# A fused attention and GeGLU kernel: from 512-token chunks with hand-placed pieces to 128-token tiles ordered by a list scheduler

## Chip, cores, metric

One core of one Trainium2 chip. The metric is the device time of one execution in microseconds (us). Each kernel was executed several times; "median" is over those executions. An execution counts as slow when it is more than 1.5% above the fastest of the same kernel; only fast ones are compared.

## The reference

A pre-LayerNorm block: multi-query attention (2048 tokens, width 640, 32 heads of 20, one K and V head shared by all), then a gated feed-forward part of width 1536. All in bf16.

```python
def _A_ref(x, wq, wk, wv, wo):            # attention; H = 32, Dh = 20
    q = (x @ wq).reshape(B, S, H, Dh).transpose(0, 2, 1, 3)
    k = x @ wk
    v = x @ wv
    scores = jnp.einsum("bhqd,bkd->bhqk", q, k) * (Dh ** -0.5)
    p = _softmax(scores, axis=-1)
    o = jnp.einsum("bhqk,bkd->bhqd", p, v)
    return o.transpose(0, 2, 1, 3).reshape(B, S, H * Dh) @ wo
def _B_ref(x, w_gate, w_up, w_down):
    return (_gelu(x @ w_gate) * (x @ w_up)) @ w_down
h  = x + _A_ref(_layernorm(x), ...)       # no affine in the LayerNorm
h2 = h + _B_ref(_layernorm(h), ...)       # (cut: rounding, shapes)
```

The exponentials set the scale: 32 x 2048 x 2048 values are 1024 instructions of 128x1024 on ScalarE.

## The kernel before

Attention runs in 512 steps. A step is one chunk of 512 queries, one group of four heads and one tile of 128 keys. A head has only 20 channels, so four heads share the matmul array in two ways. For QK each head takes 32 of the 128 rows: four matmuls with `tile_position=(32*r, 0)` run side by side (in the trace the four start within about 10 ns and are over after 0.39 us at full clock, 0.61 at half). For PV each head takes 32 of the 128 columns (0.40 and 0.62 us for the four). The kernel uses eight banks of PSUM: three pairs for scores, one for PV, and bank 7 for everything else.

```python
PAIRS = [(0, 1), (2, 3), (4, 5)]            # score banks: three slots of two
def qk_fn(e, s):                            # all four heads of a step together
    qc, g, kt = steps[s]
    pa, pb = pair_of_step[s]
    for half, pr in ((0, pa), (1, pb)):
        for rr in range(2):
            r = 2 * half + rr
            ins = e.matmul(bank(PAIRS[pr][rr]),
                kT4[32*r:32*r+32, kt*P:(kt+1)*P], qT[32*r:32*r+32, qc % 2, g, :],
                start=True, stop=True, tile_position=(32*r, 0))
    return ins
# per step: exp of pair a, exp of pair b (ScalarE, 128x1024 each),
#           qk_fn of the next step, pv_fn (four matmuls into bank 6),
#           then at most one "piece" (2 or 3 matmuls of a projection or of the FFN)
# ... (cut: pieces of one unit follow each other step by step; the FFN of the last
#      chunk runs after the attention; softmax sums by a matmul and 512-wide reciprocals)
```

The softmax here doesn't subtract the row's maximum and nothing guards it: scores larger than these inputs give would overflow.

## Time and profile before

| | before |
|---|---|
| median of 2 executions | 1118.51 us (1117.74 to 1119.27) |
| ScalarE busy | 978.6 us, 88% of the span |
| TensorE busy | 760.8 us, 68% |
| first exponential starts, last one starts | 29.6 us, 1013.5 us |
| after the last exponential | about 103 us |
| half-rate TensorE clock during the exponentials | 368 of 984 us |

The page of the profile gives each engine's busy time; then 40 equal slices of the span with the busy share of each in tenths (9 is 90% or more); PEclk is the clock granted to TensorE, in tenths of full speed. Then comes the chain of waits that ended last, by engine and line, and groups of instructions: count, then busy us and mean ns, then how long the engine stood idle before them and what released it.

```profile
PE 760.8 (68%) x5424; PEld 204.0 (18%) x5508; DVE 457.8 (41%) x693; ACT 978.6 (88%) x1088; POOL 80.4 (7%) x104
...
PE   1677666666667776666777777767766766766866
...
ACT  0799999999899999999999999999999999993030
...
PEclk9799655555899999755999999985997699966998
...
ACT 74%; DVE 16%; PE 9%; issue 1%; DMA 1%; POOL 0%; another core or an unknown queue 0%
...
L475 ACT ACTIVATE scratch_a<-ps 128x1024 bf16<-128x1024 f32 x1024 | 950.5, 1132 | 24.2 <-PE ps L462 23.3
...
L462 PE MATMUL ps<-qT,kT 32*128 32x512 bf16 x2048 | 243.0, 464 | 83.6 <-ACT scratch_a L475 77.5
```

ScalarE is the limit: it carries 74% of the chain and stands only 24.2 us before its 1024 exponentials. One lasts 1132 ns on average, but they overlap and start about every 917 ns. TensorE's clock is only half in parts of the attention, as the timeline of TensorE in such a stretch shows (columns: start, duration, engine, line, what, and how long it stood before):

```profile
200.06 0.61 PE L462 MATMUL ps<-qT,kT 32*128 32x512 bf16 x4 [0.30 <-ACT scratch_a L475]
200.98 0.62 PE L481 MATMUL ps<-scratch_a,v_ext 128*32 128x512 bf16 x4 [0.30 <-ACT scratch_a L475]
201.90 0.61 PE L462 MATMUL ps<-qT,kT 32*128 32x512 bf16 x4 [0.30 <-ACT scratch_a L475]
```

TensorE waits for ScalarE ahead of every group, even at half clock. The view of stretches of time confirms it (us busy of each engine in the stretch, then the granted clock): ScalarE is busy 10.00 of 10 us.

```profile
core 0: us, PE busy (x) PEld busy (x) DVE busy (x) ACT busy (x) POOL busy (x), PEclk, DMA share, GB/s
200.00:210.00 10.00, 6.78 (x44) 1.22 (x44) 0.00 (x0) 10.00 (x13) 0.00 (x0) 0.50 0.00 0
```

### The profile page before, as it was taken

To read this page: it belongs to the slowest core of one execution; us is meant where nothing else is said; L and a number is where in the kernel's file an instruction comes from. 1 tells how busy PE (TensorE), PEld (TensorE's weight loads), DVE (VectorE), ACT (ScalarE), POOL (GpSimd) and SP (SyncE) were. 2 spreads that over 40 slices of the span, in tenths; PEclk is the share of its full clock that TensorE was granted. 3 is DMA by queue.
4 is the path that set the end of the run, shared out by engine and by line. 5 is a ranking of instruction groups with operands and counts; after the bars stand their busy time and mean duration, and the time that the engine had idled before them with its cause. 6 is when DMAs were issued, how large, how long until landed. Compare 5 with 4: busy or idle time off the path is not lost.

```text
span 1117.3 us, 13050 instructions
## 1 busy us (share of the span) xinstructions
PE 760.8 (68%) x5424; PEld 204.0 (18%) x5508; DVE 457.8 (41%) x693; ACT 978.6 (88%) x1088; POOL 80.4 (7%) x104
## 2 busy tenths in 40 slices
PE   1677666666667776666777777767766766766866
PEld 0121111111121111111221111111221111112322
DVE  7433222211164656421224455642333356533573
ACT  0799999999899999999999999999999999993030
POOL 5200000000000111000000011100000011100130
PEclk9799655555899999755999999985997699966998
DMA  5460000000000000000000100000000000000100
GB/s 155 91 216 1 1 1 1 1 1 1 1 16 9 1 1 1 1 1 0 19 6 1 24 1 1 1 1 1 19 6 18 6 2 1 1 1 1 48 0 24
DMA packets 31772, 18.92 MB, mean 17 GB/s; under 512 B 23520, under 2 KB 30432, under 8 KB 31712
## 3 DMA queue, kind: packets, MB, share of 16 engines
q1 hardware_dynamic: 31712, 18.08, 5.9%
q8 instruction: 43, 0.70, 0.3%
q14 instruction: 17, 0.14, 0.0%
HBM read 10.21 MB, written 2.62 MB: 11 GB/s over the span
## 4 chain that ended last, share of the span: by engine, by line
ACT 74%; DVE 16%; PE 9%; issue 1%; DMA 1%; POOL 0%; another core or an unknown queue 0%
ACT scratch_a L475 72%; DVE rL_sb L527 4%; PE ps L778 2%; ACT g_th L719 2%; PE ps L672 2%; DVE g_z L713 2%; DVE hhT L733 1%; DVE g_hg L725 1%; PE ps L481 1%; PE ps L462 1%; DVE stats L277 1%; DVE stats L272 1%; PE ps L970 1%; DVE onT L531 1%; DVE xn_tmp L323 1%
## 5 line engine op out<-in xcount | busy, mean ns | idle before, releaser
L475 ACT ACTIVATE scratch_a<-ps 128x1024 bf16<-128x1024 f32 x1024 | 950.5, 1132 | 24.2 <-PE ps L462 23.3
L481 PE MATMUL ps<-scratch_a,v_ext 128*32 128x512 bf16 x2048 | 245.9, 470 | 192.9 <-ACT scratch_a L475 186.4
L462 PE MATMUL ps<-qT,kT 32*128 32x512 bf16 x2048 | 243.0, 464 | 83.6 <-ACT scratch_a L475 77.5
L481 PEld LDWEIGHTS ps<-scratch_a,v_ext 128*32 128x32 bf16 x2048 | 54.2, 95 | 382.4 <-ACT scratch_a L475 375.9
L509 DVE COPY opvT<-ps 128x512 f32<-128x512 f32 x32 | 22.1, 692 | 247.5 <-PE ps L481 247.5
L462 PEld LDWEIGHTS ps<-qT,kT 32*128 32x128 bf16 x2048 | 53.2, 94 | 313.6 <-ACT scratch_a L475 299.3
L527 DVE RECIPROCAL rL_sb<-rL_sb 128x512 f32<-128x512 f32 x32 | 107.3, 3353 | 1.1
L707 POOL TENSOR_TENSOR g_sq<-g_gs 128x512 bf16<-128x512 bf16 x48 | 53.3, 1111 | 372.1 <-DVE g_gs L700 332.5
L672 PE MATMUL ps<-xnT,wg_sb 128*128 128x512 bf16 x220 | 65.5, 401 | 15.3 <-DVE hhT L733 9.9
L672 PE MATMUL ps<-xnT,wu_sb 128*128 128x512 bf16 x228 | 66.2, 395 | 6.9 <-DVE g_gs L700 5.0
L778 PE MATMUL ps<-wd_sb,hhT 128*128 128x512 bf16 x185 | 53.6, 422 | 11.2 <-DVE hhT L733 7.2
L767 DVE CAST g_us<-ps 128x512 bf16<-128x512 f32 x36 | 24.9, 691 | 80.1 <-PE ps L672 79.7
L297 POOL TENSOR_TENSOR ln_den<-ln_ve,halfc 128x4 f32<-128x4 f32 x8 | 8.1, 1010 | 637.9 <-DVE ln_ve L295 622.6
L719 ACT ACTIVATE g_th<-g_z 128x512 bf16<-128x512 bf16 x48 | 34.6, 721 | 19.1 <-DVE g_z L713 19.1
L702 ACT ACTIVATE g_gs<-ps 128x512 bf16<-128x512 f32 x12 | 7.2, 597 | 48.5 <-PE ps L672 48.5
L525 DVE COPY rL_sb<-ps 128x512 f32<-128x512 f32 x32 | 22.0, 689 | 60.2 <-PE ps L481 53.3
L413 DVE CAST qT<-ps 128x512 bf16<-128x512 f32 x31 | 21.4, 689 | 56.6 <-PE ps L591 56.6
L700 DVE CAST g_gs<-ps 128x512 bf16<-128x512 f32 x36 | 24.8, 689 | 41.6 <-PE ps L672 41.6
L713 DVE SCALAR_TENSOR_TENSOR g_z<-g_sq,g_gs 128x512 bf16<-128x512 bf16 x48 | 39.6, 825 | 4.2 <-POOL g_sq L707 4.2
L725 DVE SCALAR_TENSOR_TENSOR g_hg<-g_th,g_gs 128x512 bf16<-128x512 bf16 x48 | 33.3, 695 | 10.9 <-ACT g_th L719 10.9
L733 DVE SCALAR_TENSOR_TENSOR hhT<-g_hg,g_us 128x512 bf16<-128x512 bf16 x36 | 31.4, 871 | 1.2
L616 PE MATMUL ps<-wo_pad,onT 128*128 128x512 bf16 x88 | 28.3, 397 | 4.9 <-DVE onT L531 3.6
(69 smaller groups left out, 362.4 us busy)
## 6 DMA issues: line engine op xcount, KB each, us to landing
xh_sb<-in_A_x_dram SPq DMA_DIRECT2D x4, 640.0 KB, 6.2
out_dram<-xh_sb SPq DMA_DIRECT2D x16, 160.0 KB, 1.8
wg_sb<-in_B_w_gate_dram SPq DMA_DIRECT2D x1, 1920.0 KB, 7.8
wu_sb<-in_B_w_up_dram SPq DMA_DIRECT2D x1, 1920.0 KB, 13.2
wd_sb<-in_B_w_down_dram SPq DMA_DIRECT2D x1, 1920.0 KB, 17.9
hhT<-in_A_wq_dram SPq DMA_DIRECT2D x1, 800.0 KB, 7.8
wo_pad<-in_A_wo_dram SPq DMA_DIRECT2D x32, 25.0 KB
xnT<-xn_tmp SPq DMA_TRANSPOSE x32, 2.6
```

What stands on the lines that cost most here:

```text
L462: ins = e.matmul(bank(PAIRS[pr][rr]), kT4[32 * r:32 * r + 32, kt * P:(kt + 1) * P], qT[32 * r:32 * r + 32, qc % 2, g, :], start=True, stop ...
L475: return e.activation(PT[s % 2][:, half * 1024:(half + 1) * 1024], src, ACT.Exp, scale=SM_SCALE)
L481: ins = e.matmul(ps[32 * hl:32 * hl + 32, 6 * 512:7 * 512], v_ext[:, kt, :], PT[s % 2][:, hl * 512:(hl + 1) * 512], start=(kt == 0), stop= ...
L527: plan.op("dve", (lambda e: e.reciprocal(rL_sb[:], rL_sb[:])), wait=[("Lcopy", gi)], mark=("recip", gi))
L616: ins = e.matmul(bank(7), onT[:, qc % 2, g, qt * P:(qt + 1) * P], wo_pad[:, g, 0:512], start=(g == 0), stop=(g == NG - 1))
L672: ins = e.matmul(bk, wsb[:, cc, fc * P:(fc + 1) * P], xnT[:, cc, tok], start=(cc == 0), stop=(cc == NC_D - 1))
L707: plan.op("pool", (lambda e: e.tensor_tensor(g_sq[:, s2(k), :], g_gs[:, s3(k), :], g_gs[:, s3(k), :], ALU.mult)), wait=[("gs", k)] + ([("z ...
L713: plan.op("dve", (lambda e: e.scalar_tensor_tensor(g_z[:, s2(k), :], g_sq[:, s2(k), :], GELU_K, g_gs[:, s3(k), :], ALU.add, ALU.mult)), wa ...
L719: plan.op("act", (lambda e: e.activation(g_th[:, s2(k), :], g_z[:, s2(k), :], ACT.Tanh, scale=GELU_C)), wait=[("z", k)] + ([("hg", kp)] if ...
L725: plan.op("dve", (lambda e: e.scalar_tensor_tensor(g_hg[:, s2(k), :], g_th[:, s2(k), :], 1.0, g_gs[:, s3(k), :], ALU.add, ALU.mult)), wait ...
L733: plan.op("dve", (lambda e: e.scalar_tensor_tensor(hhT[:, tc % 2, fc, :], g_hg[:, s2(k), :], 0.5, u_src, ALU.mult, ALU.mult)), wait=waits, ...
L778: ins = e.matmul(bk, hhT[:, tc % 2, fc, qt * P:(qt + 1) * P], wd_sb[:, fc, 0:512], start=(fc == 0), stop=(fc == NFC - 1))
```

## The change

The intent: do everything in tiles of 128 tokens, so that attention starts earlier and less work is left after it; spread all other work evenly under the exponentials; and free VectorE. Nearly every line is new. A planner simulates the engines with an assumed duration per operation and fixes, ahead of time, the order on each engine. The core:

```diff
-    PAIRS = [(0, 1), (2, 3), (4, 5)]
+    A_BANKS = [0, 2]             # scores: two slots of two banks
+    V_BANKS = [4]
+    M_BANKS = [5, 6, 7]          # projections and FFN: three banks
-    def qk_fn(e, s):             # four heads at once
+    def qk_source(e_name):       # offered to the planner whenever a slot is free
+        nu = 2                   # two heads at once: rows 0-63, then rows 64-127
+        ...
+            for i, u in enumerate(range(u0, u0 + nu)):
+                ins = e.matmul(bank(A_BANKS[tile.slot] + i), kT4[32*r:32*r+32, kt*P:(kt+1)*P],
+                    qT[32*r:32*r+32, (t//4) % 2, 4*hf:4*hf+4, (t%4)*P:(t%4)*P+P], ...
+                    tile_position=(32*r, 0))
+        o = Op("pe", fn, 300, deps, prio=-1000, acq=[tile])          # planned: 300 ns
+        ...  Op("act", ... ACT.Exp ..., 928, (o_,), prio=-1000, acq=[pt])   # planned: 928 ns
+    # FFN and projections: operations of 2 to 5 matmuls with a priority and an earliest
+    # step ("gate"); the planner puts each where TensorE would otherwise stand
+    # GELU arithmetic: VectorE -> GpSimd; softmax sums: matmul + 512-wide reciprocal ->
+    # three DMAs through DRAM + a 16-element reciprocal + a GpSimd multiply
+    # first and last tile transposed on TensorE; FFN in groups of two tiles (256 columns)
     ... (cut: about 2000 lines of diff)
```

What is the same: 1024 exponentials of 128x1024, 2048 QK and 2048 PV matmuls of 512 columns. What differs: QK now comes as two pairs of matmuls per step (each pair fills half the rows of the array), in two slots instead of three, and other work lies scattered between them.

## The prediction

> **What bounds the kernel now.** The page gives ScalarE 978.6 us busy of 1117.3 (88%), and the chain of waits is 72% the 1024 exponentials (128x1024 each). In the timeline they run at a cadence of 0.917 us although one lasts 1.115: 939 us of issue that the change does not touch. Around them: first exponential at 29.6 us (24.6 us waiting for LayerNorm and projection of 512 tokens); 36 tanh inside the loop, about 0.52 us each (19 us); 24 us of ScalarE idle waiting for QK (table of groups); last exponential ends at 1014.7; then a tail of 103 us (last chunk's projection, LayerNorm, FFN).
>
> **What the change does.** Same 1024 exponentials. It
> - starts on one 128-token tile, transposed on TensorE: first exponential at about 15 us (saves about 15); but k/v tiles now arrive through LayerNorm at about 2.2 us of VectorE per tile against 1.83 us of ScalarE per tile, so about 6 us comes back as gaps in the first pass;
> - leaves only the last tile and two late FFN groups for the tail: about 119 passes of 512 columns remain in TensorE's order after the last QK, 25 us at full clock plus the last chain of normalisation and GELU: about 38 us instead of 103 (saves about 65);
> - moves 9 more tanh under the exponentials (+5 us);
> - moves GELU arithmetic to GpSimd, the softmax sums to DMAs with a 16-element reciprocal (32 VectorE reciprocals of 3.35 us go). All off the path.
> Without new stalls: 15+6+939+23+38 = 1021 us.
>
> **What it costs: TensorE.**
> 1. QK now has two slots of two banks, where before it had three pairs. From the timeline: an exponential lasts 1.115 us, QK starts 0.06 us after it ends, and takes 0.385 us at full clock, 0.606 at half. The round trip of two slots is 1.62 us at full clock, 1.84 at half, against 1.834 for two exponentials. So at full clock there is 0.2 us of slack; at half clock none, and each projection piece ahead of a QK delays ScalarE.
> 2. The clock. The windows view shows grants of 1.0 or 0.5 only, and single low stretches last 3.41 us. [...] I counted 512-column passes per window (four tiled matmuls as one): the clock falls after windows under about 5.6, and attention alone (3.7) runs at 0.5. Before, FFN pieces came in long blocks; afterwards they are sprinkled in clusters between pure attention. QK as 2+2 counts 5.6 per window [...] (mostly warm, loss 10 to 40 us), still 3.7 if it counts array area (about a third of the windows cold, some 55 of them with projection pieces at about 1 to 1.5 us each: loss 50 to 85 us). I put both near a half.
>
> **Prediction: 1052 us**, 8 in 10 between 1025 and 1098. Faster by over 2%: 0.89; within 2%: 0.09; slower: 0.02.
>
> **What the profile would show.** Exponentials at 0.917 us cadence, first at 13 to 18 us; tail after the last one 32 to 46 us; ScalarE idle before the exponentials, released by QK, 20 to 90 us, concentrated in windows with granted clock 0.5; VectorE busy below 400 us, GpSimd near 250 us.
>
> **What would make it wrong.** The clock staying at 1.0 (near 1025); or flipping more than I think (near 1100). GpSimd's scalar operations, which have no duration in this trace, being slower than the order assumes: tanh stands at a fixed place in ScalarE's order [...]. A slower start, if weight loads delay the first tile.

Three passages are cut from the prediction: where the length of the window came from, what was thought to set the clock, and what a late tanh would do on ScalarE. None is a term of the sum, which came to 1021 us without stalls and, with 31 us added for stalls, to 1052. What the trace of the kernel before shows of the windows: its clock changes only on a grid of 3.413 us, and with the prediction's limit of 5.6 passes the count foretells 311 of 318 windows there. The 5.6 and 3.7 passes for attention alone are estimates from the spacings: three or two passes in the 1.834 us of two exponentials. The 5.6 takes each pair of QK as a whole pass, the 3.7 counts it by the share of the array that it fills; that the clock goes with the one or the other was an assumption, tested below.

## The result and the profile after

| | before | after |
|---|---|---|
| median of 2 executions | 1118.51 us | 1318.80 us (1317.30 to 1320.29) |
| ratio after to before | | 1.1793 (95%: 1.1755 to 1.1831) |
| ScalarE busy / TensorE busy | 978.6 / 760.8 us | 1018.0 / 1160.0 us |
| VectorE / GpSimd busy | 457.8 / 80.4 us | 220.3 / 266.0 us |
| mean granted clock | 0.82 | 0.63 |
| first exponential, last one starts | 29.6, 1013.5 us | 16.3, 1275.4 us |
| from the last start to the end | 103.8 us | 40.1 us |
| half clock during the exponentials | 368 of 984 us | 963 of 1259 us |

A ratio is the mean time of one kernel's fast runs over that of the other's in the same rounds, so it is not quite the ratio of the medians quoted.

The kernel is 18% slower. The page of the profile after:

```profile
PE 1160.0 (88%) x6129; PEld 342.5 (26%) x6188; DVE 220.3 (17%) x529; ACT 1018.0 (77%) x1081; POOL 266.0 (20%) x294
...
PE   5788888999997889989998888989999888999997
...
ACT  5598978788789876788767997688877898677861
...
PEclk7755566655569765575556876576556766555669
...
PE 53%; ACT 34%; DMA 5%; SPq 2%; DVE 2%; issue 2%; POOL 1%
...
L688 ACT ACTIVATE pa_sb<-ps 128x1024 bf16<-128x1024 f32 x1024 | 988.0, 1031 | 254.4 <-PE ps L673 248.0
L673 PE MATMUL ps<-qT,kT 32*128 32x512 bf16 x2048 | 545.2, 537 | 100.0 <-ACT pa_sb L688 87.7
```

Now TensorE is the limit (53% of the chain, before 9%). ScalarE stands 254.4 us before its exponentials, 248.0 of them for QK. QK's busy time went from 243.0 to 545.2 us for the same 2048 matmuls: only two instead of four run side by side (so twice the passes), and most are at half clock. The stretches show the two faces of the kernel:

```profile
core 0: us, PE busy (x) PEld busy (x) DVE busy (x) ACT busy (x) POOL busy (x), PEclk, DMA share, GB/s
320.00:360.00 40.00, 38.07 (x171) 9.76 (x172) 5.74 (x15) 28.37 (x29) 4.31 (x5) 0.50 0.06 16
720.00:760.00 40.00, 31.97 (x217) 10.57 (x218) 9.02 (x20) 37.14 (x42) 12.69 (x14) 0.91 0.05 12
```

From 320 to 360 us TensorE is busy 38.07 of 40 us *and stays at half clock throughout*; ScalarE manages 28.37. From 720 on the clock is 0.91, TensorE gets more matmuls done in less busy time, and ScalarE is busy 37.14. So the question is not "why does TensorE have more to do" but "why does a TensorE that is 95% busy not get its full clock".

Sorting the 981 spacings between neighbouring exponentials (those with a tanh between left out) by the clock at the start of the spacing shows where the time went: at full clock the excess over 917 ns sums to 25 us, at half clock to 270 us. All sums of excess below are made in this way.

### A count that predicts the clock

In the traces of the kernels before and after, the clock changes only on a fixed grid. Every clock record except the last, which ends with the trace, lasts a multiple of 3.413 us (32 records before, 77 after; the shortest, 10 and 13 of them, last 3.413 us), and each shows 1.0 or 0.5, nothing between. One step of this grid is called a window here. How long TensorE is busy in a window foretells the clock of the next one less well (at best about 88% right) than the share of the array that it fills (96%), as the following count shows.

I counted passes of 512 columns from the trace's matmul records, for each window, and asked whether the clock of the *next* window is full when the count is at or above a threshold. The count was made in two ways: by *busy time* (matmuls that run side by side are one pass, however much of the array they fill), and by *array area* (a matmul that fills a quarter of the rows or columns counts a quarter). Share of windows foretold correctly, with one threshold for all eight kernels (the others come from the experiments below; the first 20 us are left out). Two things bear on the accuracy. Each pass is taken to begin about 0.06 us after its record, a shift that was chosen because it fits. And some records of full matmuls are missing from the traces: the trace after has 6188 weight loads and 6129 matmuls.

```
threshold   count  before before_split after  k64   k64_rep m2_dummy quad2 quad2_rep | all
5.50        area   0.98   0.88         0.84   0.91  0.98    0.98     0.90  0.80      | 0.905
5.95        area   0.98   0.94         0.97   0.98  0.99    0.99     0.93  0.90      | 0.960
6.50        area   0.91   0.91         0.90   0.83  0.89    0.92     0.88  0.84      | 0.884
5.95        busy   0.98   0.73         0.59   0.98  0.99    0.94     0.93  0.90      | 0.874
7.00        busy   0.84   0.97         0.91   0.74  0.78    0.96     0.78  0.78      | 0.846
```

At 5.95 full-array passes per window, counted by area, 96.0% of all windows are right, and at least 90% in each kernel. By busy time the share is 87.4% at this threshold, with 59% in the kernel after; a recount found no threshold for busy time above about 88%. Six passes are 38% of the 15.8 that fit a window at full clock (3.413 us at the 0.216 us from start to start that the traces show).

The threshold and the shift were fitted to these windows, so the fit alone is weak proof. The recount therefore took seven kernels that are not in the table (m2, quad_late, quad2_late, norm_pe, k64_slack, k64_slack_late, before_warm; 2378 windows): the same count by area is right in 96.9% of them, by busy time at 5.95 in 84.5%. In the eight kernels of the table it gave 95.9% with the shift and 94.5% without; to say "the clock stays as it is" would be right in 80%. What the kernels don't vary is the columns: PV always comes in fours that fill them, so it is the share of the rows that is tested. The count is a fit to the records of these kernels; by what means the chip sets the clock the traces do not show.

### How a busy TensorE is held at half clock

The timeline of TensorE in the kernel after, where down-projection matmuls (L923) run between QK (L673) and PV (L721):

```profile
343.42 0.61 PE L673 MATMUL ps<-qT,kT 32*128 32x512 bf16 x2
343.96 0.62 PE L721 MATMUL ps<-pa_sb,v_ext 128*32 128x512 bf16 x4
344.51 1.03 PE L923 MATMUL ps<-wd,hh 128*128 128x512 bf16 x2
345.48 0.61 PE L673 MATMUL ps<-qT,kT 32*128 32x512 bf16 x2
346.02 1.03 PE L923 MATMUL ps<-wd,hh 128*128 128x512 bf16 x2
346.98 0.61 PE L673 MATMUL ps<-qT,kT 32*128 32x512 bf16 x2
```

None of these lines has an idle time: TensorE does not stop in this stretch. One cycle is 346.98 - 343.42 = 3.56 us and contains two QK pairs (half the array each), one PV group (the whole array) and four full matmuls: 0.5 + 0.5 + 1 + 4 = 6 full passes by area in 3.56 us. That is 6 x 3.413 / 3.56 = 5.75 per window, just under the fitted 5.95. The clock is at 0.50 throughout from 320 to 360 us, and each cycle at half clock again counts too little: I call it a trap. Two exponentials need 1.834 us; the cycle, which serves two, takes 3.56.

The trap is not perfect, and it is not all. Of the windows at half clock in the kernel after, 140 have TensorE busy for over 95% of the time: 113 of them are followed by another at half clock, 27 by one at full clock, since the mix of matmuls varies. In the kernel before there are 11 such windows, and all 11 are followed by full clock. The other half of the windows at half clock after (142) have TensorE less busy; attention without other work, at 3.7 passes per window, runs at half clock in both kernels.

With four QK matmuls at once the same work would be one QK pass in place of two, and the count would pass the fitted threshold: one QK, one PV and four full passes are 6 by area in about 0.54 + 0.55 + 3 x 0.40 + 0.57 = 2.86 us (spacings measured at half clock), 7.2 per window. That is an estimate from this trace. It fits the kernel before, whose 11 busy windows at half clock hold 6.5 to 8.0 passes by area and all lead to full clock.

The same trace shows another cost of scattering: start-to-start at full clock is 0.216 us between full passes, but 0.318 from QK to PV, 0.332 from PV to a full pass and 0.312 from a full pass to QK (medians). So here each such change of the matmul's form costs about 0.1 us; what TensorE does in that time the trace does not show. In the kernel before, the first two of these take 0.325 and 0.332 us.

### The profile page after: what moved, and what is told of

Its sections match the earlier page's. It is cut to its first block, busy times and chain, and to the rows that moved or that the text cites. A ratio compares the mean times of both kernels' runs of the same rounds, so it can differ in the third digit from the quotient of the medians.

```text
span 1315.5 us, 14670 instructions
## 1 busy us (share of the span) xinstructions
PE 1160.0 (88%) x6129; PEld 342.5 (26%) x6188; DVE 220.3 (17%) x529; ACT 1018.0 (77%) x1081; POOL 266.0 (20%) x294
## 4 chain that ended last, share of the span: by engine, by line
PE 53%; ACT 34%; DMA 5%; SPq 2%; DVE 2%; issue 2%; POOL 1%
ACT pa_sb L688 33%; PE ps L673 18%; PE ps L867 12%; PE ps L721 9%; PE ps L923 7%; PE ps L795 4%; PE ps L590 3%; SPq L410 2%; DMA rL<-lscr 1%; DMA lcol<-osb 1%; DMA lscr<-lrec 1%; POOL onT L769 1%; ACT th L890 1%; DMA xnT<-xn 1%; POOL sq L883 1%
## 5 line engine op out<-in xcount | busy, mean ns | idle before, releaser
L688 ACT ACTIVATE pa_sb<-ps 128x1024 bf16<-128x1024 f32 x1024 | 988.0, 1031 | 254.4 <-PE ps L673 248.0
L673 PE MATMUL ps<-qT,kT 32*128 32x512 bf16 x2048 | 545.2, 537 | 100.0 <-ACT pa_sb L688 87.7
L721 PE MATMUL ps<-pa_sb,v_ext 128*32 128x512 bf16 x2048 | 281.5, 541 | 3.5 <-ACT pa_sb L688 3.5
L673 PEld LDWEIGHTS ps<-qT,kT 32*128 32x128 bf16 x2048 | 102.3, 97 | 532.9 <-ACT pa_sb L688 413.8
L867 PE MATMUL ps<-xnT,wg 128*128 128x256 bf16 (+1 forms) x540 | 113.0, 371 | 0.0
L923 PE MATMUL ps<-wd,hh 128*128 128x128 bf16 (+1 forms) x370 | 105.8, 419 | 5.7 <-issue 3.3
L721 PEld LDWEIGHTS ps<-pa_sb,v_ext 128*32 128x32 bf16 x2048 | 55.4, 98 | 192.7 <-issue 183.3
L867 PE MATMUL ps<-xnT,wu 128*128 128x256 bf16 (+1 forms) x540 | 94.5, 326 | 3.4 <-POOL sq L883 3.4
L795 PE MATMUL ps<-wo_pad,onT 128*128 128x128 bf16 (+1 forms) x231 | 61.7, 386 | 16.5 <-POOL onT L769 8.4
L867 PEld LDWEIGHTS ps<-xnT,wg 128*128 128x128 bf16 x540 | 57.0, 128 | 53.2 <-issue 37.5
L895 POOL TENSOR_TENSOR hg<-th,gs 128x512 bf16<-128x512 bf16 x45 | 52.1, 1159 | 3.7
L923 PEld LDWEIGHTS ps<-wd,hh 128*128 128x128 bf16 x384 | 30.1, 116 | 53.8 <-issue 43.7
```

The source lines that it names most:

```text
L673: ins = e.matmul(bank(A_BANKS[tile.slot] + i), kT4[32 * r:32 * r + 32, kt * P:(kt + 1) * P], qT[32 * r:32 * r + 32, (t // 4) % 2, 4 * hf:4 ...
L688: ex = pl.add(Op("act", lambda e: e.activation(pa_sb[:, pt.slot, :], bank(A_BANKS[tile.slot], 2), ACT.Exp, scale=SM), 928, (o_,), prio=-10 ...
L721: ins = e.matmul(bank(V_BANKS[vt.slot])[32 * r:32 * r + 32, :], v_ext[:, kt, :], pa_sb[:, pt.slot, off:off + 512], start=(kt == 0), stop=( ...
L795: ins = e.matmul(bank(M_BANKS[tl_.slot])[:, 0:c1 - c0], onT[:, nt_.slot, g, :], wo_pad[:, g, c0:c1], start=(g == 0), stop=(g == NG - 1))
L867: ins = e.matmul(bank(M_BANKS[tl_.slot])[:, j * n:(j + 1) * n], w[:, c, fc * P:(fc + 1) * P], xnT[:, c, tok], start=(c == 0), stop=(c == N ...
L895: a6 = op(pE, (lambda gt, tt, ht_: lambda e: e.tensor_tensor(hg[:, ht_.slot, :], th[:, tt.slot, :], gs[:, gt.slot, :], ALU.mult))(gt, tt, ...
```

## Experiments

The theory and its rivals. **Area**: the clock goes with the share of the array that the matmuls of a window fill, and half-filled QK passes lower it. **Busy time**: it goes with TensorE's busy time, and falls in the kernel after for another reason, for example gaps. **Normalisation**: the softmax sums through three DMAs and GpSimd hold TensorE up. **Form**: QK in two pairs and two slots costs time whatever the clock is. The outputs of all runs were correct. The kernel before ran on the same chip, at 1118.59 to 1119.02 us median.

### k64: the same matmuls, each filling twice the rows

The contraction of each QK matmul is padded from 32 to 64 rows: K is stored in two variants, each with one of two heads' 32 rows masked to zero. Number and length of the matmuls stay; the share of the array that a pair fills goes from half to whole. Two small things change with it: the order of the heads, and VectorE copies K twice for each tile.

```diff
-    kT4 = sb("kT4", [P, S], BF16)
+    kT4 = sb("kT4", [P, 2, S], BF16)
+    kmask = sb("kmask", [P, 2], F32)      # one variant per head of a pair; evacuation of K multiplies by it
+    r = (0, 2, 1, 3)[r]
-    kT4[32*r:32*r+32, kt*P:(kt+1)*P], qT[32*r:32*r+32, ...], tile_position=(32*r, 0)
+    kT4[64*(r//2):64*(r//2)+64, r % 2, kt*P:(kt+1)*P], qT[64*(r//2):64*(r//2)+64, ...], tile_position=(64*(r//2), 0)
```

> The changed kernel with one edit: each QK matmul of a pair uses 64 array rows (two row groups, the other head's rows of the weights are zero) instead of 32, so a pair fills all four row groups in the same time and with the same order, slots and banks; two small VectorE evictions per k tile replace one. Theory A ([...] the changed kernel issues QK as two half-filled passes, so a saturated TensorE at half clock still counts under about 6 passes of 512 columns per 3.41 us window and stays at half clock): mean granted clock rises from 0.63 to 0.8 or more, ScalarE idle before the exponentials falls from 254 us to under 100 us, time 1060 to 1130 us. Rival B (two slots and the long round trip, or pieces placed ahead of QK, hold ScalarE back, whatever the clock): clock may change but time stays within 3% of 1319 us. Rival C [...]: clock and time unchanged, 1300 to 1325 us.

(Cut is what theories A and C said of the chip's workings; they are "area" and "busy time" of the list above. The "about 6 passes" are my count of the traces, 5.95 in the table. "In the same time" fits the page of k64: one QK matmul lasts 434 ns on average there; in the trace after, a pair takes 0.39 us at full clock and 0.61 at half.)

Measured: 1167.55 us (1165.46 to 1169.83), ratio to before 1.044 (1.0417 to 1.0463). From the page:

```profile
PEclk9677888697899978989788989879889897888899
...
L695 ACT ACTIVATE pa_sb<-ps 128x1024 bf16<-128x1024 f32 x1024 | 965.8, 1046 | 127.5 <-PE ps L680 124.5
```

Mean clock 0.864 (after: 0.63), half clock 314 us of the exponentials (after: 963), ScalarE's idle time halved. Time and idle time lie above what was expected (1060 to 1130 us, under 100 us), so something else is left; but 151 of the 200 us lost are back for useless multiplications by zero. TensorE has the same number of matmuls as after (6129 records in both), in nearly the same order; apart from the order of heads and the second copy of K, only the rows that QK fills differ. This is the clearest evidence for area against busy time.

### m2 and m2_dummy: more work for TensorE

A control first: one of the three banks for other work is taken away. Then that bank receives one useless full 512-column matmul after every QK pair, 1024 in all.

```diff
-    M_BANKS = [5, 6, 7]
+    M_BANKS = [5, 6]
# m2_dummy, in addition, at the end of each QK pair:
+            e.matmul(bank(7), wk4[:, 0, :], wq_pad[:, 0, 0:4, :], start=True, stop=True)
```

> Control for the next run: the changed kernel with two PSUM banks for projections instead of three, the third left unused. All theories: near the changed kernel, 1300 to 1360 us, clock 0.60 to 0.66.

> The control with one useless full-array matmul of 512 columns after every QK pair, into the unused bank: 1024 passes of work more for the busiest engine. Theory A: these passes count in full, the count per window exceeds the threshold, the clock is at 1.0 nearly always (mean over 0.9), and the kernel gets FASTER by more than 10% against the control, to 1040 to 1130 us. Rivals B and C: TensorE is already 88% busy, so 1024 passes more make it slower, over 1400 us.

(The threshold is the one counted from these traces; at 5.95 by area it foretells 98% of the windows of m2_dummy.)

Measured: control 1337.75 us (1331.54 to 1339.30), clock 0.621. With the dummies 1268.81 us (1263.98 to 1272.20), clock 0.928, ratio to before 1.1341. From the page of m2_dummy:

```profile
PE 1140.0 (90%) x7078; PEld 403.9 (32%) x7212; DVE 225.2 (18%) x529; ACT 1016.4 (80%) x1081; POOL 265.7 (21%) x294
...
PEclk9698998989989997989988898998998889988998
...
L689 ACT ACTIVATE pa_sb<-ps 128x1024 bf16<-128x1024 f32 x1024 | 987.3, 1044 | 201.1 <-PE ps L673 196.9
```

Adding 1024 useless passes makes the kernel 69 us (5%) faster than its control, where the rivals forecast over 1400 us, while the mean clock rises from 0.621 to 0.928: the time was lost at the low clock, not by too much work. But over 10% was expected, and the size was misjudged: at full clock TensorE is now really the limit (90% busy). A dummy between QK and PV adds about 0.32 us there (0.320 us from QK to the dummy and 0.320 from it to PV, in place of 0.318 from QK to PV), and 163 us of excess between exponentials remain at full clock.

### before_split: one part of the change put into the kernel before

QK of the kernel before, still in three slots, issued as two pairs, each when its own slot is free. Nothing else is changed on purpose; PV and the first pair of the step after next move ahead of the pieces.

```diff
-    def qk_fn(e, s):
+    def qk_fn(e, s, halves=(0, 1)):
         for half, pr in ((0, pa), (1, pb)):
+            if half not in halves:
+                continue
-            plan.op("pe", ... qk_fn(e, s + 1), wait=..., mark=("qk", s + 1))
+            plan.op("pe", ... qk_fn(e, s + 1, (1,)), wait=..., mark=("qk", s + 1))
+            # (0,) of step s + 2 is issued after the PV of step s, when its pair is free
```

> The kernel before with one part of the change: the four QK matmuls of a step are issued as two pairs (rows 0-63, then rows 64-127), each as soon as its own bank pair is free, with PV and the first pair ahead of the projection pieces. Slots stay three pairs, pieces stay in blocks. Theory A: attention alone stays at half clock as before and costs nothing there; blocks with pieces now spend more windows at half clock (I expect mean clock 0.65 to 0.78 instead of 0.82) and the time grows by 2 to 12%, 1140 to 1250 us. Rival B (slots and mixing are the cause, not the QK shape): within 1.5% of 1118.5 us, since slots and mixing are untouched.

Measured: two fast executions, 1204.64 and 1209.38 us; two slow ones (1233.43 and 1241.18) are not compared, so there is no interval. All four have a lower clock than before (0.685 to 0.72 against 0.82). From the page:

```profile
PEclk9799555555559799555699999665797657555898
...
L477 ACT ACTIVATE scratch_a<-ps 128x1024 bf16<-128x1024 f32 x1024 | 968.3, 1231 | 91.8 <-PE ps L464 85.3
```

Half clock 643 us against 368; the excess of spacings at half clock is 110 us, at full clock 1 us. Splitting QK alone takes the well-ordered kernel before to about +88 us. Part of the loss after therefore belongs to the form of QK, and it appears only at half clock. That speaks for area, and against form as a cost whatever the clock is. How much of it is more time at half clock, and how much the second pass of QK in that time, this run does not separate.

### quad and quad_late: QK in fours again, inside the new kernel

Three slots of two banks, QK four at once, one bank for other work.

```diff
-    A_BANKS = [0, 2]
-    V_BANKS = [4]
-    M_BANKS = [5, 6, 7]
+    A_BANKS = [0, 2, 4]
+    V_BANKS = [6]
+    M_BANKS = [7]
-        nu = 2
-        tile = Tile(pA)
+        nu = 4
+        tiles = [Tile(pA), Tile(pA)]
# (cut: order of wo and down pieces adapted to one bank). quad_late: load of wo issued after the last transpose
-    ... "wo", 820000, after=[T1[9][0]])
+    ... "wo", 820000, after=[T1[15][0]])
```

> The changed kernel's planner and order rules, but QK shaped as in the kernel before: three slots of two banks, and the four row groups' QK matmuls of a step issued together, so a step has one full QK pass instead of two half-filled ones. That leaves one PSUM bank for projections (two were freed for the third slot), so the output projection's low and high parts run one after the other and a down projection starts when its whole FFN is ready. Theory A (the shape of QK and the clock it leads to is the whole loss): mean clock at or above 0.80, ScalarE idle before the exponentials under 80 us, time 1040 to 1100 us, faster than the kernel before in spite of the single bank. Rival B (sprinkling projection pieces between attention steps is what costs): clock may rise, but time stays above 1150 us.

> The same, with the output projection's weight load queued behind the last transpose of the first LayerNorm instead of behind the tenth. In the changed kernel's trace ScalarE stands still for 10.4 us at 40 us, TensorE waiting 7.5 us for a transpose DMA issued just behind that load. If that load is the cause: 5 to 10 us faster than the run without this edit; if the transposes are late by themselves: within 2 us of it.

Measured: fast executions of quad 1195.83 to 1209.12 us (ratio 1.076), quad_late 1202.31 us (1.075). Both miss the expected 1040 to 1100 us, and they say little: I had made the second exponential of a step wait for the *completion* of the first, which took their overlap away (cadence 1.049 us in quad_late instead of 0.917). One execution of quad took 1881.81 us, and it is the one in the kept trace, which has no clock record. Of 285 spacings between neighbouring full 512-column passes, 123 are about 0.587 us and 126 about 0.84 us; the spacing at half clock is 0.426 (median in the kernel before). What held TensorE so slow is not shown. It was not seen again.

### quad2 and quad2_late: the fault mended

```diff
-                ex = pl.add(Op("act", ..., 928, (o_, prev_ex), ...))
+                ex = pl.add(Op("act", ..., 928, (o_,), after=[prev_ex], ...))
```

> The run called quad again with a fault of mine mended: there each exponential waited for the one before it to finish, and the profile shows a cadence of 1.049 us instead of 0.917. Now it is only ordered behind it. Theory A: cadence back to 0.917, worth about 0.13 us on some 980 exponentials, so 110 to 130 us off: 1065 to 1105 us, clock 0.70 to 0.85, ahead of the kernel before. Rival B (sprinkled pieces themselves cost): over 1150 us.

> The same with the output projection's weight load queued behind the last transpose of the first LayerNorm. In the faulty pair the two could not be told apart (1195 to 1209 and 1199 to 1206 us). If that load delays the first pass: 5 to 10 us faster than quad2; else within 2 us.

Measured: quad2 1180.95 us (1176.18 to 1183.12), ratio 1.0556; quad2_late 1177.99 us, 1.0535. A miss, far above 1105, and in the range of the rival, which held that the sprinkled pieces themselves cost (over 1150). The later load gained 3 us, between the two outcomes that were forecast for it. From the page of quad2:

```profile
PEclk9996666676686777977776677877668676886699
...
L690 ACT ACTIVATE pa_sb<-ps 128x1024 bf16<-128x1024 f32 x1024 | 955.8, 1060 | 150.0 <-PE ps L673 149.6
```

The cadence is back, and yet ScalarE stands 150.0 us. The form of QK is as before, so this loss belongs to another part of the change. The order is the likely one; the single bank for other work is a second (taking one of three banks away cost 19 us in m2), and no run separates them. The excess is 119 us at half clock and 31 at full clock, 24 of all this in the first 100 us. TensorE's timeline shows one stall:

```profile
300.96 0.61 PE L673 MATMUL ps<-qT,kT 32*128 32x512 bf16 x4 [0.30 <-ACT pa_sb L690]
301.51 1.25 PE L877 MATMUL ps<-xnT,wg 128*128 128x256 bf16 x5
302.68 0.62 PE L731 MATMUL ps<-pa_sb,v_ext 128*32 128x512 bf16 x4
303.23 1.05 PE L877 MATMUL ps<-xnT,wg 128*128 128x256 bf16 x5
304.21 0.40 PE L673 MATMUL ps<-qT,kT 32*128 32x512 bf16 x4
```

Attention alone makes 3.7 passes per window (estimated from the 1.834 us of two exponentials), and the clock is at half when the first FFN operation comes; it then takes 1.25 us where the plan had about 0.56, QK comes 3.25 us after the last QK instead of 1.83, and ScalarE stands for about 1 us. By the recount quad2 has 114 windows at half clock with other work in them, and they hold 92 of the 119 us; 56 of them lead to full clock. The kernel before keeps pieces in long blocks and has only 19 such windows, with 11 us.

### k64_rep: keep the clock up in quiet stretches

k64, and every second QK pair issued twice (same result) where the last seven operations on TensorE were only QK and PV.

```diff
-            for i, u in enumerate(range(u0, u0 + nu)):
+            near = pl.order["pe"][max(0, o.idx - 7):o.idx]
+            quiet = u0 % 4 == 0 and all(x.name[:2] in ("qk", "pv") for x in near)
+            for i, u in list(enumerate(range(u0, u0 + nu))) * (2 if quiet else 1):
```

> The 64-row version with every second QK pair issued twice (the same matmuls into the same banks, so the result is the same) where the preceding seven TensorE operations are attention alone. Theory A: what is left at half clock there comes from stretches of attention without projection pieces, 5.6 full passes per window, just under the threshold; the repeats lift them over it: clock from 0.86 to 0.93 or more, time 25 to 70 us below the 64-row version (1100 to 1142 us). If the threshold story is wrong: more work, time equal or longer (1165 to 1200 us).

(The 5.6 is an estimate: two QK pairs that fill the array and one PV group in 1.834 us, so 3 x 3.413 / 1.834; the threshold is the 5.95 fitted above.)

Measured: 1124.98 us (1123.83 to 1126.73), ratio 1.0055 (1.0037 to 1.0073), clock 0.938. As expected: 43 us less than k64 for 232 useless matmuls. ScalarE still stood 90.4 us. The profile's list of waits (us in total, times, longest) shows a reason:

```profile
PE ps L804 <- POOL onT L778: 25.9, 15, 2.6
PE ps L876 <- POOL sq L892: 15.0, 8, 2.6
```

TensorE, which takes its operations in the planned order, stood 25.9 us in 15 places for the normalised attention output and 15.0 us in 8 places that the list puts down to GpSimd's squares for GELU (sq), and a window in which it stands counts less. One such wait in the trace after: TensorE stands 2.05 us, until 218.97 us, for a square (sq); the QK planned behind it starts at 219.61, and ScalarE stands 2.05 us too. In k64 these waits are as long (25.6 and 16.4 us), in the kernel after 8.4 and 3.4 us.

### norm_pe: the normalisation in the kernel after

Softmax sums by matmul and reciprocal everywhere instead of by DMA (for the last half tile this path exists already).

```diff
-        if last:
+        if True:
```

> The changed kernel with one part undone: the softmax sums are spread by a TensorE matmul and a 512-element VectorE reciprocal for every half tile (as the changed kernel does for its last one), no DMA round trip through DRAM and no GpSimd multiply. All theories that blame TensorE: within 2.5% of the changed kernel, 1290 to 1350 us. If the DMA round trip or GpSimd held the chain up: faster by over 3%.

Measured: 1319.46 us (1317.72 to 1328.27), ratio 1.1813; after was 1.1793. No difference, though the clock was a little higher (0.669 in the profile against 0.63). So this rival falls for the kernel after: while TensorE is late, the normalisation is nearly in time (8.4 us of waits). The run puts matmuls in place of the DMAs, so it bounds what both together cost and not the DMAs alone. The faster k64 and k64_rep do wait for it.

### quad2_rep: the same cure for the kernel with QK in fours

The whole QK group is issued three times in quiet stretches (wo also late, so the partner is quad2_late).

```diff
+            near = pl.order["pe"][max(0, o.idx - 4):o.idx]
+            quiet = all(x.name[:2] in ("qk", "pv") for x in near)
+            for i, u in list(enumerate(range(u0, u0 + nu))) * (3 if quiet else 1):
```

> quad2_late with the QK pass of a step issued three times (same result) wherever the four TensorE operations before it are attention alone, which counts 7.4 full passes per window instead of 3.7. Theory A: clock above 0.93, ScalarE idle before the exponentials down by 15 to 40 us against quad2_late, time 1040 to 1080 us. If the clock is no longer the limit there: within 1% of quad2_late or slower.

(The 7.4 and 3.7 are estimates: four or two full passes in 1.834 us.)

Measured: 1238.28 us (1236.22 to 1246.82), ratio 1.1089, 60 us *slower* than quad2_late. A miss, and an instructive one. At half clock a window full of repeated groups lies close to the threshold on either side. The window counted from 442 us holds 18.88 QK matmuls and 4.00 of PV, each a quarter of the array: 5.72 by area, and the next window is at half clock. The one from 463 us holds 20.12 and 4.00: 6.03, and the next is at full clock. (These two counts use the shift of 0.06 us; without it they are 5.58 and 5.95.) The cure lifted the clock only from 0.75 to 0.80 in the two profiles. I think that each repetition delayed the chain where the clock stayed low: the excess at half clock rose from 120 to 157 us.

### k64_slack and k64_slack_late: a plan with true durations

The planner assumed the same latency for a group of four DMAs as for one. From the evacuation of PV to the normalised output the trace shows about 10 us (9.9 to 11.4 in eight of ten cases of k64_rep), the plan has about 7.8. So each further DMA of a group gets 450 ns. The second kernel also issues the load of wo after the last transpose.

```diff
-        return pl.add(Op("sp", fn, 2100.0 + nbytes / 180.0 + ...
+        return pl.add(Op("sp", fn, 2100.0 + 450.0 * (nd - 1) + nbytes / 180.0 + ...
# k64_slack_late, in addition
-    ... "wo", 820000, after=[T1[9][0]])
+    ... "wo", 820000, after=[T1[15][0]])
```

> k64_rep with one number of the planner changed: each DMA after the first in a group adds 450 ns to the planned duration, so that the output projection stands later in TensorE's order. If TensorE waiting for the softmax sums is what is left: that wait falls from 25 us to under 8 us and the time to 1080 to 1105 us, ahead of both kernels. If not: 1118 to 1130 us.

> The same with the output projection's weight load behind the last transpose. quad2 against quad2_late showed 3 us. If the load is what stops ScalarE for 10 us at 43 us: 6 to 12 us below k64_slack; else within 3 us.

Measured: 1068.54 us (1065.59 to 1072.47), ratio 0.9557 (0.9530 to 0.9583); and 1063.49 us (1059.41 to 1066.38), ratio 0.9509 (0.9480 to 0.9537). The first is better than its range (1080 to 1105 us); the later load gained 5 us, between the two outcomes forecast for it. The gain of k64_slack is 56 us. The waits for the normalised output fell from 25.9 to 1.2 us, and those put down to sq (15.0 us) are gone from the list too: about 40 us. I think that the rest is the low clock that each wait brought on (half clock during the exponentials is down from 137 to 82 us), but no run separates the two. One changed duration also makes the planner lay out everything behind it anew, so other moves may have a part. The page of k64_slack_late:

```profile
PE 857.1 (81%) x6383; PEld 301.3 (28%) x6440; DVE 225.4 (21%) x550; ACT 988.5 (93%) x1081; POOL 265.6 (25%) x294
...
PEclk9799999999899999999999999999999999999899
...
L697 ACT ACTIVATE pa_sb<-ps 128x1024 bf16<-128x1024 f32 x1024 | 959.8, 1049 | 32.6 <-PE ps L682 30.2
```

This version beats both kernels: 4.9% faster than before, about 19% than after. It keeps the design of the change and differs in the rows that QK fills (with the order of heads and the second copy of K), in repeated QK pairs, in one planned duration and in the place of one load. Its exponentials run from 15.8 to 1024.2 us.

### before_warm: is the clock worth anything in the kernel before?

Three useless full matmuls in each of 151 quiet steps of the kernel before, 453 in all.

```diff
+        if s > 20 and not pe_slots.get(s) and not pe_slots.get(s - 1) and bank_free[7] not in (None, OPEN):
+            plan.op("pe", dummies, wait=[bank_free[7]])      # 3 x matmul of 512 columns into bank 7
```

> The kernel before with three useless full-array matmuls in 151 attention steps that have no projection piece in them or in the step before (into the idle projection bank): 453 passes more. Clock theory: the long stretches at half clock (granted mean 0.82) go to full clock, mean 0.93 or more, and the stalls at the start of each block, most of the 24 us of ScalarE idle, shrink: 1095 to 1112 us. If the clock does not matter to this kernel: 1117 to 1125 us.

Measured: 1121.16 us (1120.20 to 1126.34), ratio 1.0038 (1.0014 to 1.0062). A miss. From the page:

```profile
PEclk9699899998899999999999999989998999998898
...
L475 ACT ACTIVATE scratch_a<-ps 128x1024 bf16<-128x1024 f32 x1024 | 950.8, 1139 | 29.0 <-PE ps L462 27.2
```

The clock rose from 0.82 to 0.944, half clock fell from 368 to 102 us, and ScalarE's idle time did not fall (29.0 against 24.2 us). In quiet attention a low clock is no cost in the kernel before: the stretch from 200 us above shows ScalarE busy all the time at 0.50, because groups of four in three slots have room at half rate: QK and PV take 0.61 and 0.62 us there, of the 1.83 us from one step to the next. Of the 31 us of excess that remain here, 21 begin in the 102 us at half clock. Whether the dummies would have gained something had they cost nothing, this run cannot tell.

## Why the prediction was wrong

**The step that failed**, as the prediction put it: "still 3.7 if it counts array area (about a third of the windows cold, some 55 of them with projection pieces at about 1 to 1.5 us each: loss 50 to 85 us)". The prediction gave this branch and the other about a half each; this one was right: by area the count foretells 96% of the windows, by busy time at best about 88%. Its size was wrong by a factor of three to five. Measured: 963 of 1259 us at half clock, not a third but three quarters, and ScalarE stood 254.4 us. The term of the sum that failed is "some 55 of them": by the recount, 208 windows at half clock had other work in them, with 251 us of excess between exponentials. That is 1.2 us each, so the price of one such window was forecast well and their number was not. I had assumed what the kernel before shows, that one window with pieces brings the clock up (13 of its 19 such windows do; after, 36 of 208). With QK in half-filled passes it doesn't: at half clock a fully busy TensorE reaches about 5.75 passes, where the fit asks for 5.95, and mostly stays there (113 of 140 windows). I had even worked out that at half clock two slots leave no slack, but had not asked what a *full* window at half clock would count.

The sum shows that little else failed. Predicted: 15 to the first exponential, 6 + 939 + 23 + 31 = 999 until the last, 38 after it: 1052 (31 is what the prediction added for stalls to its 1021). Measured in the profile: 16.3 + 1259.2 + 40.1 = 1315.6 us. Of the 264 us between them, 260 lie in the middle term.

Point by point:

- *First exponential at 13 to 18 us, tail 32 to 46 us*: right (16.3; 40.1 from the last start, about 39 after the last end). The 128-token tiles do what they were meant to do, about 77 us together.
- *Cadence 0.917 us*: right where nothing stalls (median spacing at full clock 0.904).
- *At full clock 0.2 us of slack, at half clock none*: right in direction. Excess at full clock 25 us, at half clock 270.
- *ScalarE idle 20 to 90 us*: wrong (254.4), though it is "released by QK" and "concentrated in windows with granted clock 0.5" as said.
- *VectorE below 400, GpSimd near 250 us*: right (220.3 and 266.0); and, as norm_pe shows for the sums, nearly off the path in the kernel after.
- *"Flipping more than I think (near 1100)"* named the right risk with the wrong picture: the clock doesn't flip too often, it too seldom flips back.

How much belongs to what, as far as runs show it: filling the array's rows in QK (k64) takes 151 of the 200 us back, at the same count and length of matmuls. QK in fours (quad2) takes back 138. Both leave about 50 to 60 us over the kernel before, although the head and the tail save 77: in the k64 line, k64_rep and k64_slack take 43 and 56 us off, one after the other, by more activity in quiet stretches and by a plan with more room. For quad2 no cure was found. What stays open: how the last 56 us divide into waits and clock; how much in quad2 is the order and how much the single bank; the execution of 1881.81 us; and about 42 us between k64_slack_late and the 1021 us that the prediction gave for a run without stalls; 21 us of excess between its exponentials lie in the first 100 us.

## What to carry to other kernels

In these kernels the share of the array that TensorE fills in 3.413 us foretold its clock (96% of the windows), and a TensorE busy 38.07 of 40 us stayed at 0.50. So count the work in your own trace in this way, look where the clock changes there, and ask whether a window that is *full at half clock* counts enough to leave it; here 5.75 did not. Where that happens, try tiled matmuls side by side until they fill the array, or padded so that they do (k64: 151 of 200 us back); where the limiting engine hardly waits, as in the kernel before (24.2 us), a higher clock brought nothing (ratio 1.0038). And when a scheduler spreads work evenly, check the durations it assumes against a trace: here an order that is tight at full rate turned late inputs into stalls of the engine that limits the kernel (with 450 ns more room for each further DMA, k64_slack was 56 us faster).
